# Reordering the second attention block of batch 0, one projection and the copies of values in an attention + feed-forward kernel

## The chip, the cores and the metric

The kernel runs on one core of a Trainium2 chip. The time is the device time of one execution in microseconds (us), as a median over several. The profile's span is shorter than that, 506.4 us against 508.3 for the same execution, since it runs from the first to the last instruction. All runs told here were in the fast state or, where there was a single run, of unknown state; the granted clock of the matrix engine (TensorE, PE in the profile) was 0.999 or 1.0 of full speed in every profiled run. The other engines are DVE (VectorE), ACT (ScalarE), POOL (GpSimd) and SP (SyncE, here a DMA queue).

## The reference

```python
k_proj = np.einsum('ks,bhsd->bhkd', E, k)          # batch 8, heads 8, seq 1024, head_dim 64, k_proj 64
v_proj = np.einsum('ks,bhsd->bhkd', F, v)
scores = (q @ k_proj.transpose(0, 1, 3, 2)) / 8    # softmax over the 64 projected keys
x = softmax(scores) @ v_proj                       # then heads side by side: 8192 x 512
h = x @ w_in                                       # 512 -> 2048
g = h * clip(h + 3, 0, 6) / 6
out = g @ w_out                                    # 2048 -> 512
```

## The kernel before

A batch's 1024 tokens are worked on in two blocks of 512, and its eight heads in four pairs. For each pair the kernel computes *scores* (matmuls of keys and queries, whose exponentials ScalarE takes), *sums* (the softmax denominators, as matmuls with ones), *values* (the unscaled outputs) and *products* (values times one over the sums, on VectorE). A *projection* is k_proj and v_proj of one batch, which VectorE then copies out of PSUM, the memory that TensorE writes.

Nearly all the time is the feed-forward part: 1024 matmuls with w_in and 1040 with w_out. A "first group" is four w_in matmuls into one PSUM tile, after which ScalarE and VectorE turn it into g; a "second group" is sixteen w_out matmuls into one tile, which is copied out. There are four matmul tiles (`pmm`) and four attention tiles (`pat`), each used in rotation: a new tile waits until the readers of the tile four before it are done. The attention of the next batch is cut into "visits" that stand between or inside second groups, and small copies wait in a list `later` of which one is popped after each first group.

```python
def projected(self, alloc=pat):
    self.project(alloc)             # 8 matmuls for k and 8 for v, side by side in one tile
    self.keys_out()                 # two copies on VectorE
    rest = [lambda a=a: self.values_out(a) for a in range(2)]   # two more
    if alloc == pmm:
        for r in rest:
            r()
        rest = []
    later.extend([self.turn] + rest)
# ...
# batch 0, second block: one visit for each two of the four pairs of heads
def second_values(self, j):
    js = (j, j + 1)
    den = [self.sums(1, i, pat) for i in js]        # softmax denominators
    av = [self.values(1, i, pat) for i in js]
    rec = rec_tile()
    inverse(rec, den)                               # ScalarE: log, log, exp(-log)
    for i, (j, a) in enumerate(zip(js, av)):
        nc.vector.tensor_mul(self.xT[:, j, 1, :], a, rec[:, i])
# ...
rows = [second_group(0, 0, g[0], c) for c in range(SB)]
for i in range(SB + 1):
    for c in range(SB - 1):
        next(rows[c], None)                         # four w_out matmuls of each of three groups
    if i == 0:
        first.second_scores()
    elif i < 3:
        first.second_values(2 * i - 2)
# ...
# a visit gives (inside, after): inside runs after eight of a group's sixteen matmuls
    if (b, n) == (2, 3):
        return nothing, lambda: third.projected(pmm)
# ...
```

The softmax here doesn't subtract the row's maximum and nothing guards it: scores larger than these inputs give would overflow.

Of the kernel before, what the change touches and what calls it, by code (L numbers as in the profile page):

```python
# [15 lines left out]
def kernel(  # L16
# [11 lines left out]
    nc = tc.nc  # L28
# [7 lines left out]
    KO = d_model // P  # L36
# [36 lines left out]
    def g_tile():  # L73
        return gpool.tile([P, FO, TOK], bf16, tag="g", name="g")
# [82 lines left out]
    def q_transposed(b):  # L157

        t = qT_pool.tile([P, KO, 2, TOK], bf16, tag="qT", name="qT")
        nc.sync.dma_start_transpose(t.rearrange("p j a (m n) -> p (j a m) n", n=P),  # L160
                                    kqv[b]["q"].rearrange("p h s d -> p (h s d)"))
        return t
# [3 lines left out]
    def rec_tile():  # L166
        return att.tile([P, 2, TOK], f32, tag="rec", name="rec", bufs=4)

    def log(rec, i, den):
        nc.scalar.activation(rec[:, i], den, AF.Ln)  # L170

    def inverse(rec, den=()):
        for i, d in enumerate(den):
            log(rec, i, d)
        flat = rec.rearrange("p i n -> p (i n)")
        nc.scalar.activation(flat, flat, AF.Exp, scale=-1.0)  # L176
# [5 lines left out]
    class Attention:  # L182
# [100 lines left out]
        def projected(self, alloc=pat):  # L283
            self.project(alloc)
            self.keys_out()
            rest = [lambda a=a: self.values_out(a) for a in range(2)]
            if alloc == pmm:
                for r in rest:
                    r()
                rest = []  # L290
            later.extend([self.turn] + rest)
# [63 lines left out]
    class First:  # L355
# [124 lines left out]
                    nc.scalar.activation(aT[:, r].rearrange("p i n -> p (i n)"), tiles[r],  # L480
                                         AF.Exp, scale=scale)

        def second_values(self, j):
            js = (j, j + 1)
            den = [self.sums(1, i, pat) for i in js]
            av = [self.values(1, i, pat) for i in js]
            rec = rec_tile()
            inverse(rec, den)
            for i, (j, a) in enumerate(zip(js, av)):
                nc.vector.tensor_mul(self.xT[:, j, 1, :], a, rec[:, i])  # L490


    def h_part(h_ps, xT, t, fo, kos):
# [9 lines left out]
    def first_group(xT, t, g, fo):  # L503
        h_ps = pmm()
        h_part(h_ps, xT, t, fo, range(KO))
        h_out(h_ps, g, fo)
# [5 lines left out]
    def second_group(b, t, g, c, copy=None):  # L512
        o_dst = out_rows(b, t, c)
        if (b, t, c) == (B - 1, NB - 1, SB - 1):

            for e, copy, dma in ((0, nc.vector.tensor_copy, nc.sync), (1, nc.scalar.copy, nc.scalar)):
                half = slice(e * d_model // 2, (e + 1) * d_model // 2)
                o_ps = pmm()[:, :d_model // 2]
                for fo in range(FO):
                    nc.tensor.matmul(o_ps, g[:, fo, c * P:(c + 1) * P], w_out_sb[:, fo, half],  # L520
                                     start=(fo == 0), stop=(fo == FO - 1))
                o_sb = opool.tile([P, d_model], f32, tag="o_sb", name="o_sb")[:, :d_model // 2]
                copy(o_sb, o_ps)
                dma.dma_start(out=o_dst[:, half], in_=o_sb)
            return
        o_ps = pmm()
        for fo in range(FO):
            nc.tensor.matmul(o_ps, g[:, fo, c * P:(c + 1) * P], w_out_sb[:, fo, :],  # L528
                             start=(fo == 0), stop=(fo == FO - 1))
            if fo % SB == SB - 1:  # L530
                yield
        o_sb = opool.tile([P, d_model], f32, tag="o_sb", name="o_sb")
        (copy or nc.scalar.copy)(o_sb, o_ps)  # L533
        nc.sync.dma_start(out=o_dst, in_=o_sb)

    def whole(gen):
        for _ in gen:
            pass

    def x_tile():  # L540
        return xpool.tile([P, KO, NB, TOK], bf16, tag="xT", name="xT")
# [3 lines left out]
    first = First(xT)  # L545
# [5 lines left out]
    def two_groups(xT, t, g, kos):  # L551
        tiles = [pmm(), pmm()]
        for part in kos:
            for fo in range(2):
                h_part(tiles[fo], xT, t, fo, part)
        for fo in range(2):
            h_out(tiles[fo], g, fo)
# [10 lines left out]
    def pop():  # L568
        if later:
            later.pop(0)()  # L570

    rows = [second_group(0, 0, g[0], c) for c in range(SB)]
    for i in range(SB + 1):
        for c in range(SB - 1):
            next(rows[c], None)
        if i == 0:
            first.second_scores()
        elif i < 3:
            first.second_values(2 * i - 2)
    two_groups(xT, 1, g[1], ((0, 1), (2, 3)))  # L580
    for fo in range(2, FO):
        first_group(xT, 1, g[1], fo)
# [5 lines left out]
    rest = []  # L588
# [14 lines left out]
    for b in range(1, B):  # L603
        if b + 1 < B:
            x_next = second.xT = x_tile()
        third = Attention(b + 2) if b + 2 < B else None


        def visits(b, n):
            def nothing():  # L610
                pass

            if b == 1:
                n -= SB
                if n < 3:
                    return lambda: second.visit(n, third), nothing
                return nothing, lambda: second.visit(n, third)()
            if b + 1 < B:
                six = (pmm, pmm), (pat, pat), (pat, pat)
                if (b, n) == (2, 0):  # L620
                    return lambda: second.some_scores((2, 0, 1), six), nothing
                if (b, n) == (2, 1):
                    return lambda: second.some_scores((3,), six[1:2]), nothing
                if (b, n) == (2, 3):
                    return nothing, lambda: third.projected(pmm)
                if n == 0:
                    return nothing, lambda: second.some_scores(
                        (1, 2, 3), ((pmm, pmm), (pat, pat), (pat, pmm)), third)
                if n == 2:
                    return second.sums_and_values, nothing  # L630
                if n == 5:
                    return second.first_products, nothing
                if n == 6:
                    return lambda: second.last_values(third), nothing
            return nothing, nothing

        for t in range(NB):
            if b == 1 and t == 1:
                qT_dma[3] = q_transposed(3)
            g = g_tile()  # L640
            for fo in range(FO):
                if b < 3 and t == 0 and fo < 2:

                    if fo == 0:
                        two_groups(xT, t, g, ((0, 1, 2), (3,)))
                else:
                    first_group(xT, t, g, fo)
                pop()
                if b == 1 and t == 0 and fo == 10:
                    second.projected()  # L650
                if not behind or fo % SB < SB - 1:
                    continue
                inside, after = visits(b, t * SB + fo // SB)
                rows = second_group(*behind[0], fo // SB, nc.vector.tensor_copy if b == 1 else None)
                next(rows)
                next(rows)
                rest = inside()
                whole(rows)
                after()
                if rest:  # L660
                    rest()
            behind = [(b, t, g)]
        second, xT = third, x_next
# [32 lines left out]
```

## Time and profile before

| what | value | where |
|---|---|---|
| time | 508.95 us, median of 3 (508.8 to 509.43) | timed runs |
| span, PE busy | 506.4 us, 99% | the page's first part |
| ACT, DVE busy | 51%, 49% | the same |

The measure is the *step*, the time from one matmul's start to the next's. PEld in the views stands for TensorE's weight loads, one for each matmul.

### The profile page before, as it was taken

The numbers are of one execution on the slowest core, as the hardware profiler recorded it, in microseconds if no ns is written. First come the engines' busy times: TensorE is split into PE (matmuls) and PEld (weight loads), VectorE is DVE, ScalarE is ACT, GpSimd is POOL, SyncE is SP. The second block draws the span as 40 slices with busy tenths as digits, with TensorE's granted clock in tenths as the row PEclk, the third lists the DMA queues.
The fourth block names the chain that finished last, engine by engine and source line by source line (L and its number), as shares of the span: only waits on it lengthen the run. The fifth ranks groups of instructions, "written<-read, shape, count | busy, mean of one in ns | idle before, by whom it ended". The sixth has DMA issues, their size and how long they took to land.

```text
span 506.4 us, 7084 instructions
## 1 busy us (share of the span) xinstructions
PE 499.8 (99%) x2779; PEld 225.3 (44%) x2779; DVE 246.2 (49%) x384; ACT 256.2 (51%) x438; POOL 37.9 (7%) x57
## 2 busy tenths in 40 slices
PE   8999999999999999999999999999999999999997
PEld 4444444444444444444444444444444444444444
DVE  3572836865733564536635455534652446334420
ACT  3656466567565444654555544654455544434431
POOL 8610020020020020010002000000000000000000
PEclk9999999999999999999999999999999999999999
DMA  9999999599299998699316990248110361101112
GB/s 168 200 205 207 204 153 238 104 151 190 86 154 187 271 150 168 137 160 256 107 43 130 215 263 30 60 99 208 41 43 29 84 159 43 41 22 42 43 42 83
DMA packets 77529, 66.02 MB, mean 130 GB/s; under 512 B 36200, under 2 KB 66664, under 8 KB 77496
## 3 DMA queue, kind: packets, MB, share of 16 engines
q0 software_dynamic: 31952, 29.36, 37.1%
q1 hardware_dynamic: 45320, 35.82, 27.1%
q10 hardware_dynamic: 224, 0.39, 0.3%
q8 instruction: 21, 0.34, 0.3%
q14 instruction: 12, 0.10, 0.1%
HBM read 69.73 MB, written 16.94 MB: 171 GB/s over the span
## 4 chain that ended last, share of the span: by engine, by line
PE 96%; ACT 2%; DVE 1%; issue 0%; ACTq 0%
PE mm L528 43%; PE mm L495 43%; PE at L195 2%; PE mm L93 1%; PE at L244 1%; PE at L226 1%; PE mm L244 1%; PE mm L520 1%; PE mm L264 1%; ACT aT L235 0%; PE at L382 0%; PE at L414 0%; PE mm L226 0%; PE at L394 0%; PE mm L195 0%; PE at L366 0%
## 5 line engine op out<-in xcount | busy, mean ns | idle before, releaser
L501 DVE SCALAR_TENSOR_TENSOR g<-r,mm 128x512 bf16<-128x512 f32 x256 | 174.5, 687 | 176.3 <-ACT r L500 175.6
L495 PE MATMUL mm<-xT,w_in_sb 128*128 128x512 bf16 x1024 | 231.0, 379 | 0.3
L528 PE MATMUL mm<-w_out_sb,g 128*128 128x512 bf16 x1008 | 230.4, 379 | 0.2 <-DVE g L501 0.2
L500 ACT ACTIVATE r<-mm 128x512 f32<-128x512 f32 x256 | 152.3, 599 | 76.9 <-PE mm L495 75.7
L495 PEld LDWEIGHTS <-w_in_sb 128*128 128x128 bf16 x1024 | 99.3, 98 | 122.6 <-issue 4.0
L528 PEld LDWEIGHTS <-g 128*128 128x128 bf16 x1008 | 96.8, 98 | 120.3 <-issue 7.0
L533 ACT COPY o_sb<-mm 128x512 f32<-128x512 f32 x55 | 32.1, 586 | 124.0 <-PE mm L528 124.0
L257 DVE TENSOR_TENSOR xT<-at,rec 128x512 bf16<-128x512 f32 x42 | 26.5, 682 | 6.5 <-ACT rec L176 6.5
L235 ACT ACTIVATE aT<-at 128x512 bf16<-128x512 f32 x38 | 20.2, 615 | 9.1 <-PE at L226 9.1
L201 DVE CAST kp<-at 64x512 bf16<-64x512 f32 x12 | 7.7, 677 | 15.5 <-PE at L195 15.5
L216 POOL COPY mark<-qT 1x1 bf16<-1x1 bf16 x4 | 0.7, 177 | 161.6 <-DMA qT<-q 161.6
L235 ACT ACTIVATE aT<-mm 128x512 bf16<-128x512 f32 x18 | 10.3, 613 | 3.6 <-PE mm L226 3.6
L533 DVE COPY o_sb<-mm 128x512 f32<-128x512 f32 x8 | 5.5, 687 | 13.4 <-PE mm L528 13.4
L195 PE MATMUL at<-v,f_t 128*64 128x512 bf16 x48 | 11.5, 382 | 0.0
L195 PE MATMUL at<-k,e_t 128*64 128x512 bf16 x48 | 11.5, 382 | 0.0
L257 DVE TENSOR_TENSOR xT<-mm,rec 128x512 bf16<-128x512 f32 x14 | 9.0, 685 | 4.3 <-PE mm L244 4.3
L176 ACT ACTIVATE rec<-rec 128x1024 f32<-128x1024 f32 x10 | 10.6, 1061 | 0.3
L170 ACT ACTIVATE rec<-mm 128x512 f32<-128x512 f32 x10 | 5.5, 595 | 7.9 <-PE mm L244 5.4
L93 PE MATMUL mm<-ones 128*128 128x512 bf16 x19 | 7.8, 539 | 1.5 <-DVE halves L84 1.5
L170 ACT ACTIVATE few<-mm 128x512 f32<-128x512 f32 x10 | 5.4, 594 | 7.4 <-PE mm L264 7.4
L195 PEld LDWEIGHTS <-e_t 128*64 128x64 bf16 x56 | 5.6, 109 | 6.6 <-issue 1.9
L204 DVE CAST vp<-at 64x512 bf16<-64x512 f32 x12 | 8.3, 694 | 0.4
(75 smaller groups left out, 161.9 us busy)
## 6 DMA issues: line engine op xcount, KB each, us to landing
out_dram<-o_sb SPq DMA_DIRECT2D x63, 256.0 KB, 2.7
rec<-rows SPq DMA_DIRECT2D x40, 256.0 KB, 6.3
k<-in_k_dram POOLq DMA_DIRECT2D x7, 1024.0 KB, 14.2
v<-in_v_dram POOLq DMA_DIRECT2D x7, 1024.0 KB, 21.1
q<-in_q_dram POOLq DMA_DIRECT2D x7, 1024.0 KB, 10.3
w_out_sb<-in_moe_w_out_dram POOLq DMA_DIRECT2D x4, 512.0 KB, 17.3
k<-in_k_dram POOLq DMA_DIRECT2D x4, 256.0 KB, 5.4
v<-in_v_dram POOLq DMA_DIRECT2D x4, 256.0 KB, 7.7
```

Source lines behind the costliest of these rows:

```text
L93: nc.tensor.matmul(ps, ones[:, :P], ones, start=True, stop=True)
L170: nc.scalar.activation(rec[:, i], den, AF.Ln)
L176: nc.scalar.activation(flat, flat, AF.Exp, scale=-1.0)
L195: nc.tensor.matmul(ps[e * KP:(e + 1) * KP], ef_t[e][:, so, :], kqv[self.b]["kv"[e]][:, :, so, :], start=(so == 0), stop=(so == SO - 1))
L235: nc.scalar.activation(self.aT[j][:, r].rearrange("p a n -> p (a n)"), tiles[r], AF.Exp, scale=scale)
L244: nc.tensor.matmul(tiles[t][c:c + D].rearrange("p (r n) -> p r n", r=2), stationary(r, 2 * j + a), self.aT[j][r:r + KP, :, a, :], start=Tr ...
L257: nc.vector.tensor_mul(self.xT[:, j, t, :], av[t], rec[:, t])
L495: nc.tensor.matmul(h_ps, w_in_sb[:, ko, fo * P:(fo + 1) * P], xT[:, ko, t, :], start=(ko == 0), stop=(ko == KO - 1))
L500: nc.scalar.activation(r, h_ps, AF.Relu, bias=0.5, scale=1.0 / 6.0)
L501: nc.vector.scalar_tensor_tensor(g[:, fo, :], r, 1.0, h_ps, op0=ALU.min, op1=ALU.mult)
L528: nc.tensor.matmul(o_ps, g[:, fo, c * P:(c + 1) * P], w_out_sb[:, fo, :], start=(fo == 0), stop=(fo == FO - 1))
L533: (copy or nc.scalar.copy)(o_sb, o_ps)
```

## The change

The second block of batch 0 takes the sums of all four pairs in one visit and all values in the next, so that the values wait for ScalarE and no longer for VectorE's products. The projection of batch 4 moves from behind a w_out group to its middle, so that its copies run beside eight more matmuls. The two copies of a projection's values, until now one first group apart, get two empty turns between them.

```diff
-            rest = [lambda a=a: self.values_out(a) for a in range(2)]
+            rest = [lambda: self.values_out(0), lambda: None, lambda: None, lambda: self.values_out(1)]
...
-        def second_values(self, j):
-            js = (j, j + 1)
-            den = [self.sums(1, i, pat) for i in js]
-            av = [self.values(1, i, pat) for i in js]
-            rec = rec_tile()
-            inverse(rec, den)
-            for i, (j, a) in enumerate(zip(js, av)):
-                nc.vector.tensor_mul(self.xT[:, j, 1, :], a, rec[:, i])
+        def second_sums(self):
+            self.recs = [rec_tile() for _ in range(KO // 2)]
+            den = [self.sums(1, j, pat) for j in range(KO)]
+            for i, rec in enumerate(self.recs):
+                inverse(rec, den[2 * i:2 * i + 2])
+
+        def second_values(self):
+            av = [self.values(1, j, pat) for j in range(KO)]
+            for j in range(KO):
+                nc.vector.tensor_mul(self.xT[:, j, 1, :], av[j], self.recs[j // 2][:, j % 2])
...
-        if i == 0:
-            first.second_scores()
-        elif i < 3:
-            first.second_values(2 * i - 2)
+        if i < 3:
+            (first.second_scores, first.second_sums, first.second_values)[i]()
...
-                    return nothing, lambda: third.projected(pmm)
+                    return lambda: third.projected(pmm), nothing
```

## The prediction

> **What bounds the kernel now.** I read the page first, then the chain of work that ended last in order of time, then the waits of the matrix engine, and last the timeline around each place where the chain leaves that engine. From the page:
>
> ```profile
> PE 499.8 (99%) x2779; PEld 225.3 (44%) x2779; DVE 246.2 (49%) x384; ACT 256.2 (51%) x438; POOL 37.9 (7%) x57
> PE 96%; ACT 2%; DVE 1%; issue 0%; ACTq 0%
> ```
>
> PE is busy for 499.8 of 506.4 us and 96% of the chain is PE; no other engine is above 51%. So only time in which PE stands still, or work taken off PE, can move the end. The busy figure doesn't show how much it stands still, because a matmul's recorded end is modelled. The chain does, since there a run of matmuls lasts as long as it really took:
>
> ```profile
> 48.45 6.91 PE mm L495 x32
> 96.39 8.02 PE mm L495 x36
> 416.04 3.45 PE mm L528 x16
> ```
>
> The first number is the start, the second the length. 3.45 / 16 = 6.91 / 32 = 0.216 us is the undisturbed step of one 128x512 matmul. The run of 36 should last 36 x 0.216 = 7.77 us and lasts 8.02: 0.25 us too long. I went through the starts of all 2779 matmuls for steps over 0.245 us. After 21 us, when the pipeline is full, there are two kinds. Some sixty are 0.31 us, each where the kind of tile changes (128x128 to 64x64 or 128x64, or back). Five are longer: 0.50 us at 45, 0.36 at 102, 0.52 at 168.5, 0.53 and 0.57 at 385 to 387. The diff touches the first three.
>
> At 45 us, the second block of batch 0, the second visit of the old code:
>
> ```profile
> 42.92 1.06 ACT L176 ACTIVATE rec<-rec 128x1024 f32<-128x1024 f32 x1
> 44.01 1.29 DVE L490 TENSOR_TENSOR xT<-at,rec 128x512 bf16<-128x512 f32 x2 [6.92 <-ACT rec L176]
> 44.85 0.91 PE L414 MATMUL at<-aT,vp 64*64 64x512 bf16 x4
> 45.35 0.10 PEld L414 LDWEIGHTS <-vp 64*64 64x64 bf16 x1 [0.49 <-issue]
> ```
>
> The four attention PSUM tiles are all taken: two by the new sums, two by the values of the pairs before, which VectorE frees only with its products. These end at 44.01 + 1.29 = 45.30, and the last value goes at 45.35. The page calls the wait "issue", but the 0.05 us from the product's end tells whose it was.
>
> At 168.5 us, the projection of batch 4:
>
> ```profile
> 166.09 3.94 PE L495 MATMUL mm<-xT,w_in_sb 128*128 128x512 bf16 x16
> 167.54 1.40 DVE L204 CAST vp<-mm 64x512 bf16<-64x512 f32 x2
> 168.97 2.48 DVE L501 SCALAR_TENSOR_TENSOR g<-r,mm 128x512 bf16<-128x512 f32 x4
> 168.99 0.55 PEld L495 LDWEIGHTS <-w_in_sb 128*128 128x128 bf16 x4 [0.63 <-DVE vp L204]
> 173.32 3.62 PE L495 MATMUL mm<-xT,w_in_sb 128*128 128x512 bf16 x16
> ```
>
> Four copies of the projection run 166.23 to 168.94; its tile is one of four matmul tiles, and the fourth group after it needs it back. The sixteen matmuls take 3.94 us where a clean sixteen takes 3.62 on the same view: 0.32 lost (0.30 by the step, 0.519 - 0.216).
>
> At 102 us, the projection of batch 2:
>
> ```profile
> 99.61 0.69 DVE L204 CAST vp<-at 64x512 bf16<-64x512 f32 x1
> 100.33 0.69 DVE L501 SCALAR_TENSOR_TENSOR g<-r,mm 128x512 bf16<-128x512 f32 x1
> 101.05 0.69 DVE L204 CAST vp<-at 64x512 bf16<-64x512 f32 x1
> 101.78 3.12 DVE L501 SCALAR_TENSOR_TENSOR g<-r,mm 128x512 bf16<-128x512 f32 x5
> ```
>
> A group comes every 4 x 0.216 = 0.863 us and costs VectorE 0.69; with a copy it costs 1.38. Two in a row put it over a microsecond behind. The product that starts at 101.78 ends at 102.47, and PE goes on at 102.52 instead of 102.38. That is 0.14 us of the excess of 0.25 above; the rest is one tile change.
>
> **What the Trainium skill says.** "TensorEngine Tiling (Array Packing)", Key Properties: changing the tiling mode drains TensorE. The trace agrees: 0.309 us against 0.216 at a change, so 0.093 each. "TensorE: Matmul & The Clock Gate", section "Wait — 56ns, not 53.3ns?", gives 215.7 ns between warm matmuls of 512 columns, start to start; the trace has 0.216. "ScalarE: Activation LUTs", section "What ACT_TABLE_LOAD costs", says that back-to-back ACTIVATEs overlap by about 93 ns; here the two logs start at 41.80 and 42.30 and last 0.60 each, an overlap of 0.10. "Perfetto Trace Analysis", Optimization Strategies, advises to work on whichever engine keeps the matmul engine waiting; that is the change's intent, and the three waits above are what is there to gain.
>
> **The change part by part.** The instruction lists of both programs hold the same 5560 entries on PE, and the same number on each other engine. Nothing is added or removed; only order and waits change. The matmul work stays as it is.
>
> *Sums in one visit, values in the next.* Each visit remains eight 64x64 matmuls of 512 columns, four tiles side by side, with one tile change in and one out: nothing gained or lost there. The sums of all pairs go at 41.36; their four tiles come free from the exponentials, which end at 40.62. The values then wait for ScalarE's logs, not for VectorE's products. ScalarE in its new order: logs at 41.80 and 42.30, inverse 42.92 to 43.98, third log from 43.88 to 44.48, fourth log from 44.37 to 44.97 (durations from the trace, starts with the 0.10 overlap). Values of pairs 0 and 1 go at 44.61 as now, pair 2 at 44.85; pair 3 waits until 44.97 + 0.05 = 45.02, where now the last value goes at 45.35. Gain: **0.33 us**. A wait of about 0.16 stays, because the first inverse stands ahead of the last two logs. Behind it, the second inverse ends at 46.05 and the four products by about 47.5, and PE wants the last two pairs at 47.96 + 0.86 = 48.8: free.
>
> *Batch 4's projection after eight of the sixteen matmuls of a w_out group.* Same two tile changes. The projection ends about 1.8 us earlier (164.1 instead of 165.9), the copies run 164.5 to 167.2 beside the other eight matmuls, and the first product of the next groups is ready only at 167.8 (group from 166.09, 0.65 to the last start, 0.38 for that matmul, 0.65 for the ACTIVATE). The fourth group wants the projection's tile at 166.09 + 3 x 0.863 = 168.7, 1.4 us after it is free. Gain: **0.30 us**. The data is there: v of batch 4 is issued at 140.41 and lands 16.0 us later, at 156.4, against 162.5 when it is now wanted.
>
> *Copies of values two groups further apart.* This touches the projections of batches 1, 2, 5, 6 and 7. With one copy the next product is some 0.5 us late, and a group has about 1.1 us of slack before its tile is wanted (3.45 us for four groups, less 2.36 from start to freed tile). So the wait at 102 goes: **0.14 us**. In the others a w_out group of 3.45 us follows soon and no step is long today, so they give nothing. The second copies still come well before the values are used.
>
> Sum: 0.33 + 0.30 + 0.14 = **0.77 us** of 508.95, or 0.15%, so about **508.2 us**.
>
> **The rivals.** (1) *The fourth log takes the whole place of the product.* If ScalarE starts the third log only after the inverse, without overlap, and hands over slowly, the wait in the values visit is 0.3 and not 0.16, and the gain 0.6 us: 508.35. For it: the wait does move to ScalarE. Against: it overlaps in this very stretch. (2) *The gain is given back later.* If PE, 0.8 us early, met a transfer, the time would stay at 508.9. For it: the DMA row is full until 45 us, and w_out's last chunk is wanted right after the visits. Against: that chunk lands at 42.5, three microseconds early; k and v of batch 1 land at 51.9 and are wanted at 55.3; PE's list of waits names no DMA at all after that. (3) *The projection inside an open accumulation costs something*, a wait for a tile still being read, say. For it: w_out's tile and the projection's are both held, which leaves two for the next groups. Against: those two are long free, and the third, w_out's own, is copied by about 166.9 and wanted at 167.8. It would cost 0.3 to 1 us: 508.5 to 509.2. (4) *Late copies of values hold the attention tile* that a following visit needs; that visit is over 8 us away in each case, so I give it little.
>
> **Range and chances.** All the time in which PE stands still and which the change can reach is 0.50 - 0.01 + 0.30 + 0.14, under 1 us; 2% would be 10 us. Nothing in the diff can lose 10 us without a wait of a kind that the program doesn't hold. The three runs of before spread over 0.6 us, as much as the whole effect, so the range follows more from that than from the steps: 507.5 to 508.9. Chances: faster by over 2% 0.005, within 2% 0.99, slower 0.005.
>
> **What would show it right or wrong.** In the values visit, the step before the last pair should be near 0.16 us and end 0.05 after the fourth log; in the old place of the products no wait is left. The sixteen w_in matmuls after batch 4's projection should take 3.62 us as clean ones do, and the run of 36 at 96 us 7.87. PE's tile changes should be as many as before, and the two waits at 385 to 387 us untouched. The profiled span should fall from 506.4 to about 505.6. I am wrong if one of the three waits keeps its length, if a new step over 0.35 us appears, or if the span doesn't move though they are gone.

## The result, and the profile after

The changed kernel takes 507.75 us (median of 6, 507.4 to 507.99) against 508.88 us of before (median of 6, 507.95 to 509.43). The ratio is 0.9979 with a 95% interval of 0.9966 to 0.9992: within 2%, and clear of 1. Ratios here are those that the measurement gives over the fast runs of both kernels; they are not quite the ratios of the quoted medians. A second set of five rounds gave 507.72 against 508.6, ratio 0.998 (0.9966 to 0.9993).

The first profile of the changed kernel lacks fifty matmul records (2729 instead of 2779, visible on its page), which shows as steps of 0.43 us, twice 0.216. Three profiles further down (copies together, logs first, last scores split) lack fifty as well. The weight loads are complete in all, so I compared those, and took a second profile of the same kernel, from the second set of rounds, which is complete. Its page:

```profile
span 505.5 us, 7084 instructions
PE 499.2 (99%) x2779; PEld 225.0 (45%) x2779; DVE 245.0 (48%) x384; ACT 256.4 (51%) x438; POOL 37.9 (8%) x57
PE 97%; ACT 1%; DVE 0%; issue 0%; ACTq 0%
```

The chain has a per cent more of PE and a per cent less each of ACT and DVE. These are rounded shares, and part of them is the start; what the change did is read from the chain itself. In the chain of waits of the same profile, in order of time (start, length, what), the places of the three waits read:

```profile
44.58 0.72 PE at L414 x8
48.00 6.91 PE mm L497 x32
96.00 7.88 PE mm L497 x36
165.74 3.45 PE mm L497 x16
```

The run of 36, 8.02 us before, now takes 7.88, which is 36 x 0.216 and one tile change. The sixteen behind batch 4's projection take a clean 3.45. The values visit is eight matmuls in one piece of 0.72 us, with no detour over another engine between them. The waits near 385 us, which the change doesn't touch, are there as before (0.53 and 0.57 in the first profile of after).

The timeline of the first profile around the values visit shows what is left there (columns: start, length, engine, line, operation, and the idle time before it):

```profile
43.26 1.06 ACT L176 ACTIVATE rec<-rec 128x1024 f32<-128x1024 f32 x1
44.22 1.06 ACT L170 ACTIVATE rec<-at 128x512 f32<-128x512 f32 x2
44.95 0.79 PE L414 MATMUL at<-aT,vp 64*64 64x512 bf16 x8
45.34 0.10 PEld L414 LDWEIGHTS <-vp 64*64 64x64 bf16 x1 [0.25 <-issue]
```

The third and fourth log start 0.1 us before the inverse ends and end at 44.22 + 1.06 = 45.28; the last pair's values go at 45.34. Before, the last pair waited for a product.

And around batch 4's projection:

```profile
164.28 1.90 PE L530 MATMUL mm<-w_out_sb,g 128*128 128x512 bf16 x8
164.42 1.28 DVE L201 CAST kp<-mm 64x512 bf16<-64x512 f32 x2 [2.29 <-PE mm L195]
165.73 1.40 DVE L204 CAST vp<-mm 64x512 bf16<-64x512 f32 x2
167.71 0.69 DVE L503 SCALAR_TENSOR_TENSOR g<-r,mm 128x512 bf16<-128x512 f32 x1 [0.58 <-ACT r L502]
```

The four copies, 164.42 to 167.13, lie beside the other eight w_out matmuls, and the first product behind them finds VectorE idle for 0.58 us.

**A measure without the start.** The profiled spans fell by 0.4 us (first profile) and 0.9 us (second). Both mix the effect with a start that varies from execution to execution: the first w_in weight load came at 20.70 us in the profile of before, at 21.04 and 20.59 in the two of after. So from here on I use the *stretch* from the first w_in weight load to the start of the last matmul: 482.11 us before, 481.37 and 481.37 after. That is a gain of **0.74 us**. Comparing the weight loads one by one says where:

| place | gain |
|---|---|
| values visit, 45 us | 0.35 |
| batch 1's score visit, 68 us | -0.06 |
| run of 36 w_in matmuls, 96 to 104 us | 0.14 |
| batch 4's projection, 168 us | 0.31 |
| sum | 0.74 |

The loss at 68 us was not expected. In the timeline of VectorE ahead of that visit, before:

```profile
65.75 0.69 DVE L501 SCALAR_TENSOR_TENSOR g<-r,mm 128x512 bf16<-128x512 f32 x1 [2.47 <-ACT r L500]
66.61 0.69 DVE L501 SCALAR_TENSOR_TENSOR g<-r,mm 128x512 bf16<-128x512 f32 x1 [0.18 <-ACT r L500]
```

and after, with the visit itself:

```profile
66.45 0.69 DVE L204 CAST vp<-at 64x512 bf16<-64x512 f32 x1
67.18 1.88 DVE L503 SCALAR_TENSOR_TENSOR g<-r,mm 128x512 bf16<-128x512 f32 x3
68.45 0.47 PE L226 MATMUL mm<-qT,kT 64*64 64x256 bf16 x8
```

The spacing pushed batch 1's second copy past a w_out group, to just before the visit. Its products run back to back behind it (1.88 us for three), a matmul tile comes free late, and the first scores take 0.47 us instead of 0.41. The second of the three products ends at 68.47; in the third part's own run below it ends at 68.45, and the second score matmul starts at 68.51.

### The profile page after: what moved, and what is told of

It is laid out like the page before. It is cut to its first block, busy times and chain, and to the rows that moved or that the text cites. A ratio compares the mean times of both kernels' runs of the same rounds, so it can differ in the third digit from the quotient of the medians.

```text
span 506.0 us, 7034 instructions
## 1 busy us (share of the span) xinstructions
PE 495.5 (98%) x2729; PEld 225.1 (44%) x2779; DVE 245.1 (48%) x384; ACT 256.3 (51%) x438; POOL 37.9 (8%) x57
## 4 chain that ended last, share of the span: by engine, by line
PE 94%; DMA 2%; POOL 2%; issue 1%; ACT 1%; DVE 0%; ACTq 0%; POOLq 0%
PE mm L530 43%; PE mm L497 43%; PE at L195 2%; DMA v<-in_v_dram 2%; PE at L244 1%; PE at L226 1%; PE mm L244 1%; PE mm L522 1%; POOL q L106 1%; PE mm L264 1%; POOL k L110 1%; ACT aT L235 0%; PE mm L226 0%; POOL v L110 0%; PE mm L195 0%
## 5 line engine op out<-in xcount | busy, mean ns | idle before, releaser
L530 PE MATMUL mm<-w_out_sb,g 128*128 128x512 bf16 x985 | 227.8, 379 | 1.9 <-issue 1.0
L257 DVE TENSOR_TENSOR xT<-at,rec 128x512 bf16<-128x512 f32 x42 | 26.5, 682 | 6.5 <-ACT rec L176 6.5
```

The source lines that it names most:

```text
L257: nc.vector.tensor_mul(self.xT[:, j, t, :], av[t], rec[:, t])
L530: nc.tensor.matmul(o_ps, g[:, fo, c * P:(c + 1) * P], w_out_sb[:, fo, :], start=(fo == 0), stop=(fo == FO - 1))
```

## The experiments

Every kernel gave correct results. Each row below rests on one profile, but for the changed kernel's two, which agree within 0.01 us. The profile decides, since effects of 0.1 to 0.4 us lie below the spread of the timed runs, 0.5 to 2 us. Beside the stretch, the comparison of weight loads between two profiles gives the place of each difference.

| kernel | stretch, us | expected | first w_in load at |
|---|---|---|---|
| before | 482.11 | | 20.70 |
| changed, two profiles | 481.37, 481.37 | | 21.04, 20.59 |
| first part alone | 481.77 | 481.75 | 20.52 |
| second part alone | 481.80 | 481.81 | 21.04 |
| third part alone | 482.03 | 482.03 | 20.67 |
| changed, one empty turn | 481.30 | 481.31 | 21.21 |
| changed, copies together | 481.57 | about 481.5 | 20.79 |
| changed, logs first | 481.41 | 481.22 | 20.83 |
| changed, last scores split | 481.22 | 480.9 | 20.60 |
| three mends together | 480.72 | 480.7 to 481.1 | 21.07 |
| and later projection | 480.78 | 480.71 | 20.45 |

### Each part alone

Before, with the sums and values reordered and the other two lines as they were:

```diff
 # the changed kernel, with
-rest = [lambda: self.values_out(0), lambda: None, lambda: None, lambda: self.values_out(1)]
+rest = [lambda a=a: self.values_out(a) for a in range(2)]
-return lambda: third.projected(pmm), nothing
+return nothing, lambda: third.projected(pmm)
```

> The kernel before with the first part alone (all sums in one visit, all values in the next). Measure: the stretch from the first w_in weight load to the last matmul, which leaves the start out; it is 482.11 us before and 481.37 after. Theory (three separate waits of the matrix engine, each removed by its own part): the step in front of the last pair's values near 45 us falls from 0.50 to about 0.15, the waits near 102 (0.36) and 168.5 us (0.52) keep their lengths, the stretch falls by 0.36 to 481.75; the visit near 68 us stays undisturbed, as before. Rival (the gain of after is luck of the start or of the run): the stretch is 482.1 here too. Rival for the small new delay of 0.06 us near 68 us in after: if it comes from the matrix engine being early rather than from the late copy, it shows here.

The stretch is 481.77. The step in front of the last pair is about 0.15 us; the one near 102 is 0.361, the one near 168 is 0.522, and the visit near 68 shows no delay. So the first part is worth 0.35 us, by itself, and being early does not cause the delay at 68. The timed runs could not have told: 509.18 us (median of 4) against 508.29, ratio 1.0013 with an interval of 0.9991 to 1.0034. Two of its four runs lie near 509.8, and I have no profile of those.

Before, with the projection inside the group:

```diff
-return nothing, lambda: third.projected(pmm)
+return lambda: third.projected(pmm), nothing
```

> The kernel before with the second part alone (batch 4's projection after eight of the sixteen matmuls of a w_out group). Theory: the step of 0.52 us near 168.5 becomes 0.22, the sixteen w_in matmuls behind take 3.62 instead of 3.94, no new step appears inside the split w_out group apart from its two tile changes of 0.31; the stretch falls by 0.30 to 481.81. Rival (a projection inside an open accumulation costs a wait of its own): a step over 0.35 us inside that group and a gain under 0.15.

From the chain of waits of this run:

```profile
161.21 1.73 PE mm L528 x8
162.94 1.85 PE mm L195 x16
164.79 1.83 PE mm L528 x8
166.62 3.45 PE mm L495 x16
```

Eight, projection, eight, and sixteen clean ones. The two tile changes are 0.309 and 0.311 us and no other step in the group is long. The gain is 0.31 and an open accumulation costs nothing extra: the rival falls. Timed: 508.16 against 508.29, ratio 0.9996 (0.9978 to 1.0014).

Before, with the spacing:

```diff
-rest = [lambda a=a: self.values_out(a) for a in range(2)]
+rest = [lambda: self.values_out(0), lambda: None, lambda: None, lambda: self.values_out(1)]
```

> The kernel before with the third part alone (two empty turns between the two copies of values). Theory: the step of 0.36 us near 102 becomes 0.22 (gain 0.14), and the visit near 68 us, before which the second copy of batch 1 now falls, starts its second score matmul some 0.06 us late, because the products behind that copy free their matmul tiles late; net gain 0.08, stretch 482.03. Rival (prediction: in the other batches the spacing costs nothing): no delay near 68, net gain 0.14, stretch 481.97.

The gain at 102 is 0.138 us, the loss at 68 is 0.060. From its chain:

```profile
96.43 7.88 PE mm L495 x36
```

So the third part nets 0.08 us and brings its own loss; the rival, which is what I had predicted, falls. Timed: 508.28 against 508.29, ratio 1.0001 (0.9984 to 1.0018). The three parts alone give 0.35 + 0.31 + 0.08 = 0.74 us, which is all of the change: they don't interact.

### How far apart the copies must be

One empty turn in place of two:

```diff
-rest = [lambda: self.values_out(0), lambda: None, lambda: None, lambda: self.values_out(1)]
+rest = [lambda: self.values_out(0), lambda: None, lambda: self.values_out(1)]
```

> The changed kernel with one empty turn between the copies instead of two. Theory: one turn is enough, as a single copy puts VectorE only about 0.5 us behind and a group has 1.1 us of slack: the step near 102 stays 0.22; and batch 1's second copy falls ahead of a whole w_out group instead of ahead of the visit near 68, so the delay of 0.06 there goes: stretch 481.31 against 481.37 of after. Rival (two turns are needed): a step of 0.25 to 0.35 near 102 comes back.

Nothing comes back at 102, and the loss at 68 is gone (0.063 us earlier behind that visit). In the timeline of this run the copy is at 62.62, ahead of a whole w_out group, and the scores take their 0.41 again:

```profile
62.62 0.69 DVE L204 CAST vp<-at 64x512 bf16<-64x512 f32 x1
68.62 0.41 PE L226 MATMUL mm<-qT,kT 64*64 64x256 bf16 x8
```

Both copies in one turn:

```diff
+rest = [lambda: (self.values_out(0), self.values_out(1))]
```

> The changed kernel with both copies of values in one turn, back to back. It tests the arithmetic of slack: VectorE is put 1.38 us behind at once, and a group has 1.1. Theory: the wait near 102 comes back, one group earlier (near 101.3) and as a step of 0.35 to 0.45 us; the delay near 68 goes, since batch 1's copies fall early; stretch about 481.5. Rival (only the number of copies within a window matters, not their spacing, or the wait had another cause): no step over 0.25 near 101 to 103.

The step appears at 101.04 to 101.52 us: 0.48, a little more than the 0.35 to 0.45 expected. On VectorE:

```profile
99.35 1.40 DVE L204 CAST vp<-at 64x512 bf16<-64x512 f32 x2
100.78 3.12 DVE L503 SCALAR_TENSOR_TENSOR g<-r,mm 128x512 bf16<-128x512 f32 x5
```

The product behind the copies ends about 0.69 us after 100.78, at 101.47, and PE goes on at 101.52. So the dose decides: 1.40 us of copies at once makes a wait of 0.27 us, the same two copies one group apart 0.14, two groups apart none. That agrees with the prediction's estimate of 1.1 us of slack per first group: 1.40 less 1.1 is 0.3.

### The wait left in the values visit

```diff
-for i, rec in enumerate(self.recs):
-    inverse(rec, den[2 * i:2 * i + 2])
+for j in range(KO):
+    log(self.recs[j // 2], j % 2, den[j])
+for rec in self.recs:
+    inverse(rec)
```

> The changed kernel with ScalarE taking all four logs before the two inverses. Theory (the wait left in the values visit is for the fourth log, which stands behind the first inverse of 1.06 us): the step of 0.15 us in front of the last pair goes, stretch 481.37 - 0.15 = 481.22; the products come later but well before the w_in matmuls want them. Rival (the wait is the matrix engine's own, of the tile change or of the weights): the step stays 0.15.

The visit gets 0.168 us shorter, against 0.15 expected; the wait was for the fourth log behind the first inverse. But the stretch is 481.41, not shorter at all. The gain is given back at 55 us, in batch 1's projection:

```profile
54.90 0.40 PE L195 MATMUL at<-k,e_t 128*64 128x512 bf16 x1
55.14 0.38 PE L195 MATMUL at<-v,f_t 128*64 128x512 bf16 x1
55.14 0.40 PE L195 MATMUL at<-k,e_t 128*64 128x512 bf16 x1
```

The k and v halves, which otherwise start within 0.004 us of each other, start 0.24 apart. v of batch 1 was issued at 27.39 and took 27.7 us, so it landed at 55.1. In the profile of before it landed at 53.8, and PE came for it at 55.3. So PE came 0.4 us sooner here and v landed 1.3 us later.

The later landing goes with the first part of the change: in the three profiles without it (before, second and third part alone) v lands at 53.8, in the nine with it between 54.45 and 55.3. In those nine the first write of results to DRAM is issued earlier too, at 46.6 to 47.5 us against 47.7 to 48.1, because ScalarE, done with its logs, makes the copy for it sooner; more of its transfer then runs beside that of v, before v has landed. That this is the cause was not tested.

### The two waits at 385 us

Batch 7's scores of three pairs, in one visit before, over two visits and in attention tiles alone:

```diff
+if third is None and n < 2:
+    js, four = (((1, 2), six[1:]), ((3,), six[1:2]))[n]
+    return nothing, lambda: second.some_scores(js, four)
 if n == 0:
     return nothing, lambda: second.some_scores(...)
```

> The changed kernel with batch 7's scores of three pairs spread over two visits (two pairs, then one), all in attention tiles. Theory: the two steps of 0.53 and 0.57 us near 385 to 387 come from six exponentials of 0.5 us in a row on ScalarE ahead of the next groups' ACTIVATEs, while in the batches before a projection of 1.85 us gives ScalarE time to catch up; with four and then two, both steps become 0.22: gain 0.66, less one more pair of tile changes (0.19): stretch 480.9. Rival (the four matmul tiles are the shortage, not ScalarE's time): the steps shrink because these scores take no matmul tile; then the same result with ScalarE's queue still over 1 us behind.

There the program gains 0.43 us (0.22 in the first visit, 0.31 and 0.35 in the two waits, less 0.45 for the added visit and its tile changes), against 0.47 expected. The stretch, 481.22, gains only 0.15: the rest is lost at 55 us, where v of batch 1 is waited for again (k at 54.84, v at 55.15). The mend is not to blame. The second profile of the changed kernel had as quick a start (20.59 against 20.60), and its PE came for v at the same 54.84; but there v had landed at 54.72, and here it landed at 55.10.

By the times, my theory and its rival each had one of the two waits. In the timeline of before, behind that visit:

```profile
382.93 3.94 PE L495 MATMUL mm<-xT,w_in_sb 128*128 128x512 bf16 x16
385.13 0.66 ACT L235 ACTIVATE aT<-mm 128x512 bf16<-128x512 f32 x1
386.31 2.48 DVE L501 SCALAR_TENSOR_TENSOR g<-r,mm 128x512 bf16<-128x512 f32 x4 [6.19 <-ACT r L500]
```

The fourth group starts at 385.84, 0.05 us after the exponential of a score that sat in a matmul tile (385.13 + 0.66 = 385.79): a tile held, though that exponential, too, stood behind five others. The w_out group starts at 387.05, just after the first product, which ScalarE's row of six exponentials had made late: a late engine. The run takes both away at once, so which of the two was at work in each wait, and how much each would give alone, is read from the times and not tested.

### All mends together

Three kernels in the same five rounds: the changed kernel again, all three mends on top of it (logs first, one empty turn, scores split), and the same with batch 1's projection one first group later, so that v has landed.

> The changed kernel once more, beside the next two, so that they share the runs of before. Stretch from the first w_in weight load to the last matmul: 481.37 as in the first profile, or up to 0.3 more if the start is quick and v of batch 1, which lands near 54.5 to 55.1 us, is then waited for. Time: 0.7 us under before if the steps hold (ratio 0.9986); the rival, that the first ratio of 0.9979 was the size of the effect, asks for 1.1 us under.

> The changed kernel with the three mends together: all logs first, one empty turn between copies, batch 7's scores in two visits. Theory: the gains add to 0.17 + 0.06 + 0.43 = 0.66, stretch 480.71, but up to 0.4 is given back where the matrix engine meets v of batch 1, which it now reaches 0.17 us earlier; so 480.7 to 481.1, and in time 0.3 to 0.65 us under the changed kernel. Rival (a wait on the data of batch 1 was chance in two runs): 480.71 flat.

> As v4_all, with batch 1's projection one w_in group (0.86 us) later, so that v has landed when the matrix engine comes to it. Theory: no staggered start of the projection's two halves; stretch 480.71 if the transposed queries of batch 1, which then land some 0.4 us later, are still in time for the scores near 67.8 us; a rival is that these scores now wait for them, which shows as a step over 0.35 us ahead of the visit near 68.

```diff
-if fo == 7:
+if fo == 8:
     second.projected()
```

| kernel | median of 5, us | ratio to before (508.6) | 95% interval |
|---|---|---|---|
| changed | 507.72 | 0.998 | 0.9966 to 0.9993 |
| three mends | 507.08 | 0.9969 | 0.9957 to 0.9982 |
| and later projection | 507.14 | 0.9968 | 0.9955 to 0.9981 |

The mends add up: the stretch fell by 0.17 + 0.06 + 0.43 = 0.66, to 480.72. This profile had a late start, 21.07, and no wait for v: PE came at 55.15, and v had landed at about 54.7 (issued at 27.63, 27.1 us). With the later projection the start was quick, 20.45, and the halves of the projection still begin together (55.390 and 55.394). The copy that falls before the visit near 68 costs its 0.06 us again there, since it moves with the projection; the scores don't wait for the transposed queries. Its profiled span is the shortest of all, 504.8 us; in time the two versions can't be told apart. Both beat the changed kernel in their medians by 0.6 us, though their intervals overlap with its.

## Why the prediction was right, and where it was not

The time, 507.75, lies in the range, and the traces bear out the mechanism of all three parts.

1. *Sums and values*, said 0.33 us, measured 0.35. The wait that stays was put at 0.16 and is 0.15, and it is for the fourth log, as said; the first rival (no overlap on ScalarE) fell.
2. *Projection inside the group*, said 0.30, measured 0.31. No new step, as said.
3. *Spacing*, said 0.14, measured 0.14 at 102 us. But "In the others a w_out group of 3.45 us follows soon and no step is long today, so they give nothing" was wrong for batch 1. That sentence looked at the old places of the copies. The new place of the second one is on the other side of the w_out group, with a visit right behind it, and there it costs 0.06 us. So the term is 0.08 and not 0.14, and two empty turns are one too many. The fourth rival was given little because the visit is "over 8 us away in each case"; for batch 1 it begins 1.3 us behind the copy (67.15 to 68.45), and what it waits for is a matmul tile that the late products hold, not the attention tile.
4. *"k and v of batch 1 land at 51.9"* was misread from the landings: in the profile of before the last piece of v landed at 27.26 + 26.5 = 53.8 us, and PE's margin was 1.5 us, not 3.4. Nor was the DMA row full only "until 45 us": in the view of the first 60 us it is full to about 58. And the sum left out that the change itself would move v's landing: it came at 54.45 and 54.72 in the two profiles of the changed kernel, and PE's margin fell to 0.8 and 0.12 us. So for this change the second rival stayed a rival, in one profile narrowly. In two variants it became real: once with PE 0.17 us earlier (logs first), and once with PE no earlier than in the changed kernel, when v landed later (last scores split).
5. *The sum*, said 0.77, measured 0.74 by the stretch. It is closer than its terms, which were 0.03 too small in the first two and 0.06 too large in the third; that is luck. The medians differ by 1.1 us in the first set and by 0.9 in the second. Their intervals, 0.9966 to 0.9993 together, hold the 0.9985 that 0.74 us make, so I don't claim that more was gained. The spans of all timed executions are on record too, and in the second set their medians agree with the stretches: 506.7 us before, 506.0 changed and 505.3 with three mends, so 0.7 and 1.4 us less, against 0.74 and 1.39. What else moves is the start: in the profiled executions the first w_in load came anywhere from 20.45 to 21.21 us, whatever the kernel.
6. *The span* was to fall to 505.6; the two profiles have 506.0 and 505.5, with the start in between.
7. *"Some sixty"* tile changes of 0.31 us: the trace has 54, of 0.30 to 0.33. Nothing rests on it.

## What to carry to other kernels

In a kernel that one engine fills to 99%, list that engine's start-to-start steps and take each step that is too long back to the instruction that ended 0.05 us before it; here the change was worth the sum of what it took off three such steps, less what it put on at another place. When work is spaced out, look at what stands behind its new place as well as what it leaves. And every gain brings the engine closer to the transfers that it now finds landed, and may start other transfers sooner beside them; so compute each margin from issue and time to landing, and again after the change, before counting on the next gain.

## What the Trainium skill lacked or had wrong

- "TensorEngine Tiling (Array Packing)", Key Properties, says that a change of mode drains TensorE, with no figure. Here a change costs 0.093 us, 0.309 against 0.216, alike into 64x64 and 128x64 tiles and out of them.
- "ScalarE: Activation LUTs", What ACT_TABLE_LOAD costs: 186 ns + 0.833 ns per element (immediate scale and bias) gives, as an estimate, 612 ns for 512 elements and 1039 for 1024. Measured are 592 to 597 (a log that reads PSUM) and 1057 (an exponential within SBUF). The overlap of two in a row was 0.10 us, against about 93 ns on the page.
- "TensorE: Matmul & The Clock Gate", The HAM clock gate, says that the moment at which the clock opens varies from run to run. That agrees: eight transposes near 7 us came every 0.107 us in the profile of before and every 0.061 in the first of after, 0.25 us earlier in all. No page speaks of the other variation of the start seen here, a last piece of v of batch 0 that lands at 18.2 us in before and at 19.7 in the first profile of after, and holds PE up by 0.59 us.
- No page has the time from the release of a PSUM tile to the matmul that waits for it; it was 0.05 us at 45, 101, 102 and 385 us.
